# Four transposed chunks per PSUM bank in the first projection of a DiT block: earlier transposes, a reused bank, and one more split

## The chip, the cores, the metric

The kernel is one block of a diffusion transformer, written by hand for one core of one Trainium2 chip. The metric is the device time of one launch, in microseconds, lower is better. Every kernel here was correct against the reference. In all traces but one (x2_late, below) the granted clock, the share of full speed that the profile shows for the matrix engine, was 1.00 between 8.4 and 26 us, where the change lives.

Names: PE is the matrix engine (PEld its loading of weights), DVE the vector engine, ACT the scalar engine, POOL a further one; SP issues loads. PSUM is the memory into which the kernel's matmuls write, SBUF the one that holds their operands. A load "lands" when its last data have arrived.

## The reference, cut to what matters

```python
mod = (silu(c) @ w_mod).reshape(B, 6, 1, D)             # shift_a, scale_a, gate_a, ...
h   = layernorm(x) * (1 + scale_a) + shift_a            # B=2, N=256, D=1152
qkv = h @ wqkv                                          # k first in this kernel, then q, v
...                                                     # attention, wo, gate, second norm, MLP with F=4608
```

Only the first lines matter here. The kernel computes K from `layernorm(x) * (1 + scale_a)` while the weights are still arriving, and adds the shift later. D is nine chunks of 128, so the K projection is nine "K steps"; each needs one chunk of the normalized x, transposed, times its scale.

## The kernel before

The tokens are four tiles of 128: tiles 0 and 1 are batch 0, tiles 2 and 3 are batch 1. For each chunk the matrix engine transposes x into PSUM, DVE (batch 0) or ACT (chunk 1 and up, alternating) multiplies by the scale and writes `hT0` in SBUF, and the matrix engine multiplies `hT0` with six column blocks of `w_k`, accumulating in six PSUM banks. The two other banks are a rotating pair ("aux") for transposed chunks and for the scale matmuls (`scale_group`: nine matmuls of two columns per chunk).

```python
def scale_group(k0, k1, tile_of=aux_tile):              # pm = silu(c) @ w_scale for chunks k0..k1
    pm = tile_of([P, k1 - k0, B], "pm")
    ...                                                 # 9 matmuls of 2 columns per chunk
def modulate(pt, i, k, b, j0, eng):                     # hT0[chunk k, batch b] = pt * scale_a
    ...
# ---- the stage, in program order (cut) ----
pt_a = transpose_x([0, 1], BT[0])                       # chunks 0-1 of batch 0
act_mean_eps(2); act_root(2); root_exp(2, 3)            # statistics of token tile 2, on ACT
norm1(3, 0, CUT)
pm0, pm1 = [scale_group(k, k + 1, acc_tile) for k in range(2)]
...                                                     # hT0 chunks 0 and 1 of batch 0, on DVE
norm1(2, 0, CUT)                                        # DVE: x of tile 2, normalized, chunks 0-3
pt_c = aux_tile([P, 2, N], "pt", BF16)
transpose_x([0, 1], [3], pt_c, 1)                       # tile 3
fill(1)                                                 # one matmul on zeros, keeps the engine busy
k_step(0, 0, N)
k_step(1, 0, N, 0, 2)
transpose_x([0, 1], [2], pt_c, 0)                       # tile 2, the last to be normalized
k_step(1, 0, N, 2)
modulate(pt_c, 0, 0, 1, 0, "d"); modulate(pt_c, 1, 1, 1, 0, "a")
norm1(0, CUT, D); norm1(1, CUT, D)
k_step(0, N, T)
pm = scale_group(2, 4)
pt_b = transpose_x([2, 3], BT[0])
scale_add(pm, 2, 4)
modulate(pt_b, 0, 2, 0, 0, "d"); modulate(pt_b, 1, 3, 0, 0, "a")
norm1(2, CUT, D)
k_step(1, N, T)
pt_d = transpose_x([2, 3], BT[1])
...
k_step(2, 0, N); k_step(2, N, T)
for k in range(3, KD):
    split = 2 if k == 5 else 0
    k_step(k, 0, T, 0, split)                           # two of six column blocks first
    if k in (3, 5, 7):
        k1 = min(k + 3, KD)
        scale_add(scale_group(k + 1, k1), k + 1, k1)    # scales of the next two chunks
    if k < KD - 1:
        both(transpose_x([k + 1], range(NT)), k + 1)    # transposes, then DVE batch 0, ACT batch 1
    k_step(k, 0, T, split)
```

The loads of x (288 KB each) are the first on SP's queue, in the order tile 0, 1, 3, 2; the weights follow.

## Time and profile before

| | before |
|---|---|
| time, median of 6 runs | 243.49 us (243.23 to 243.89) |
| span of the profiled run | 241.4 us |
| matrix engine busy | 236.4 us, 98% |
| the stage of the change | 8.6 to 25.5 us |

From the page of the kernel before, the busy times and the chain that ended last:

```profile
PE 236.4 (98%) x1688; PEld 145.1 (60%) x1698; DVE 91.4 (38%) x193; ACT 59.9 (25%) x121; POOL 28.3 (12%) x47
...
PE 94%; issue 2%; ACT 2%; POOL 1%; DVE 0%; POOLq 0%; DVEq 0%; ACTq 0%
```

Busy time can't show whether the matrix engine waits, because matmuls overlap: each is listed for its whole passage. So I read start-to-start distances. Here is the timeline of PE of the kernel before, cut to the stretch that the change rewrites (columns: start in us, time until the end of the last of the group, engine, source line, operation, output<-inputs, shapes, count):

```profile
11.03 0.29 PE L264 MATMUL pt<-ident,xn 128*128 128x128 bf16 x2
11.15 1.42 PE L280 MATMUL pk<-big,w_k 128*128 128x256 bf16 x10
12.41 0.59 PE L247 MATMUL pm<-sT,w_scale_a 128*128 128x2 bf16 x18
12.86 0.38 PE L264 MATMUL pt<-ident,xn 128*128 128x128 bf16 x4
13.08 0.82 PE L280 MATMUL pk<-big,w_k 128*128 128x256 bf16 x6
13.74 0.39 PE L264 MATMUL pt<-ident,xn 128*128 128x128 bf16 x4
13.96 1.47 PE L280 MATMUL pk<-big,w_k 128*128 128x256 bf16 x12
15.27 0.59 PE L247 MATMUL pm<-sT,w_scale_a 128*128 128x2 bf16 x18
15.73 0.38 PE L264 MATMUL pt<-ident,xn 128*128 128x128 bf16 x4
...
17.24 0.39 PE L264 MATMUL pt<-ident,xn 128*128 128x128 bf16 x4
17.46 1.89 PE L280 MATMUL pk<-big,w_k 128*128 128x512 bf16 x8
```

One 256-column matmul of L280 is listed with 0.27 us, so twelve of them in 1.47 us start every (1.47 - 0.27) / 11 = 0.109 us. In the same way a transpose takes its turn of 0.055 us, a two-column matmul 0.025, a 512-column one 0.216. The Trainium skill, "TensorE: Matmul & The Clock Gate", section "Wait — 56ns, not 53.3ns?", gives N / 2.4 GHz + 2.5 ns and a floor of 25 ns; the trace agrees at all four sizes. Wherever the distance is longer, the engine waited. (In some groups a record is missing, and the distance doubles for that reason alone; those I leave out.) Read like this, the matrix engine of the kernel before waits 0.29 us ahead of the tile 2 transposes at 11.03, 0.17 us within the ten matmuls from 11.15.

Two landmarks will serve as a ruler: **the start of the tile 2 transposes** (11.03) and **the start of K step 4** (17.46), 6.43 us apart.

### The profile page before, as it was taken

How to read it: one execution, taken by the hardware profiler on the slowest of the kernel's cores; microseconds unless marked ns; L12 is line 12 of the kernel's file. 1: busy time of each engine (PE TensorE's matmuls, PEld its weight loads, DVE VectorE, ACT ScalarE, POOL GpSimd, SP SyncE). 2: the span in 40 equal slices, each digit the busy share in tenths (PEclk: the TensorE clock that was granted, in tenths of full speed). 3: DMA queues.
4: the chain of work that ended last, by engine and by line, in shares of the span. 5: the costliest groups of instructions: out<-in, count | busy, mean ns of one | idle time of the engine just before them, and what ended most of it. 6: DMA issues, size and time to landing. Idle time of an engine off the chain costs nothing.

```text
span 241.4 us, 3978 instructions
## 1 busy us (share of the span) xinstructions
PE 236.4 (98%) x1688; PEld 145.1 (60%) x1698; DVE 91.4 (38%) x193; ACT 59.9 (25%) x121; POOL 28.3 (12%) x47
## 2 busy tenths in 40 slices
PE   8999999999999999999999999999999999999994
PEld 5775444466667665888844444444665566666574
DVE  4842442319325678930003999950010000000001
ACT  6723322307215032770423333222000000000000
POOL 2300000001300324100000000001121111111111
PEclk9999999999999999999999999999999999999999
DMA  6999999997499993739999999999300000000000
GB/s 196 325 317 311 377 366 391 391 391 244 122 331 394 389 274 76 195 65 378 391 391 391 337 326 270 287 327 270 98 16 16 20 16 16 19 18 20 26 21 16
DMA packets 48781, 53.29 MB, mean 221 GB/s; under 512 B 9587, under 2 KB 36475, under 8 KB 48763
## 3 DMA queue, kind: packets, MB, share of 16 engines
q1 hardware_dynamic: 41312, 50.14, 62.5%
q10 hardware_dynamic: 6939, 1.71, 4.6%
q0 software_dynamic: 512, 1.19, 1.8%
q8 instruction: 13, 0.21, 0.4%
q14 instruction: 5, 0.04, 0.1%
HBM read 50.14 MB, written 1.19 MB: 213 GB/s over the span
## 4 chain that ended last, share of the span: by engine, by line
PE 94%; issue 2%; ACT 2%; POOL 1%; DVE 0%; POOLq 0%; DVEq 0%; ACTq 0%
PE pacc L802 29%; PE pacc L746 29%; PE pacc L693 7%; PE pacc L599 7%; PE pq L521 7%; PE pk L280 5%; PE pk L309 2%; PE pa L640 2%; PE ps_s L556 2%; PE pn L416 2%; ACT sink L206 1%; PE pt L264 1%; PE pm L247 1%; PE pg L498 0%; ACT rstd L335 0%
## 5 line engine op out<-in xcount | busy, mean ns | idle before, releaser
L746 PE MATMUL pacc<-hT,w_f 128*128 128x256 bf16 (+1 forms) x427 | 70.3, 325 | 0.3
L802 PE MATMUL pacc<-w_f,gT 128*128 128x384 bf16 (+2 forms) x468 | 70.5, 314 | 0.0
L802 PEld LDWEIGHTS <-gT 128*128 128x128 bf16 x468 | 44.4, 98 | 26.3
L746 PEld LDWEIGHTS <-w_f 128*128 128x128 bf16 x432 | 42.2, 98 | 27.6
L808 DVE TENSOR_TENSOR tmp<-pacc,gate 128x384 f32<-128x384 f32 (+2 forms) x13 | 6.8, 526 | 65.6 <-PE pacc L802 57.0
L778 ACT ACTIVATE gT<-pacc 128x512 bf16<-128x512 f32 x24 | 14.3, 597 | 32.7 <-PE pacc L746 32.7
L469 DVE SCALAR_TENSOR_TENSOR part<-w_gate_m,s,part 128x1152 f32<-128x1152 bf16 x16 | 21.4, 1412 | 0.0
L810 POOL TENSOR_TENSOR o_sb<-tmp,x 128x384 bf16<-128x384 f32 (+1 forms) x12 | 11.7, 972 | 53.9 <-DVE tmp L808 53.9
L693 PE MATMUL pacc<-w_o,big 128*128 128x384 bf16 x108 | 17.9, 326 | 0.0
L521 PE MATMUL pq<-hT,w_q 128*128 128x512 bf16 x79 | 17.7, 379 | 0.1
L599 PE MATMUL pacc<-w_v,hT 128*128 128x384 bf16 x108 | 17.7, 326 | 0.0
L599 PEld LDWEIGHTS <-hT 128*128 128x128 bf16 x108 | 10.5, 98 | 7.1 <-issue 0.2
L693 PEld LDWEIGHTS <-big 128*128 128x128 bf16 x108 | 10.4, 98 | 7.2 <-issue 0.4
L521 PEld LDWEIGHTS <-w_q 128*128 128x128 bf16 x81 | 7.8, 98 | 9.4
L280 PE MATMUL pk<-big,w_k 128*128 128x256 bf16 (+1 forms) x70 | 13.1, 324 | 0.1
L699 POOL TENSOR_TENSOR x<-tmp,x_sb 128x384 f32<-128x384 f32 x8 | 7.3, 912 | 27.0 <-DMA w_scale_m<-in_w_mod_dram 15.0
L467 DVE TENSOR_SCALAR part<-w_gate_m,s 128x1152 f32<-128x1152 bf16 x2 | 1.6, 818 | 21.9 <-DMA w_gate_m<-in_w_mod_dram 21.9
L491 POOL DMA_DIRECT2D gates_dram<-nat_v x2 | 1.1, 534 | 67.7 <-DVE nat_v L489 67.7
L280 PEld LDWEIGHTS <-w_k 128*128 128x128 bf16 x72 | 6.7, 97 | 3.7 <-issue 0.3
L767 ACT ACTIVATE gT<-pacc 128x512 bf16<-128x512 f32 x12 | 6.5, 598 | 9.1 <-PE pacc L746 9.1
L173 PE MATMUL pwarm<-zeros 128*128 128x256 f32 x18 | 7.4, 587 | 1.2 <-DVE eps_t L93 1.2
L512 POOL DMA_DIRECT2D gates_dram<-nat x4 | 2.4, 604 | 49.6 <-DVE nat L509 48.5
(102 smaller groups left out, 165.0 us busy)
## 6 DMA issues: line engine op xcount, KB each, us to landing
w_f<-in_w_fc_dram SPq DMA_DIRECT2D x12, 864.0 KB, 14.1
w_f<-in_w_fc_dram SPq DMA_DIRECT2D x3, 1728.0 KB, 7.9
w_f<-in_w_fc_dram SPq DMA_DIRECT2D x2, 2592.0 KB, 17.4
w_gate_a<-in_w_mod_dram SPq DMA_DIRECT2D x3, 864.0 KB, 12.1
w_v<-in_wqkv_dram SPq DMA_DIRECT2D x3, 864.0 KB, 13.8
w_o<-in_wo_dram SPq DMA_DIRECT2D x3, 864.0 KB, 14.0
w_shift_m<-in_w_mod_dram SPq DMA_DIRECT2D x3, 864.0 KB, 8.6
w_scale_m<-in_w_mod_dram SPq DMA_DIRECT2D x3, 864.0 KB, 13.3
```

The source lines that it names most:

```text
L173: nc.tensor.matmul(dst[:, 0:T // 2], zeros32[:, 0:P], zeros32, start=True, stop=True)
L280: nc.tensor.matmul(pk[m][:, c0:c1], w_k[:, k, m * P:(m + 1) * P], hT0[:, k, c0:c1], start=(k == 0 and c0 == 0), stop=(k == KD - 1), skip_g ...
L469: nc.vector.scalar_tensor_tensor(part[:, b, :], wg[:, k, :], s32[:, k, b:b + 1], part[:, b, :], op0=ALU.mult, op1=ALU.add,)
L521: nc.tensor.matmul(pq[m][:], w_q[:, k, m * P:(m + 1) * P], hT[:, k, :], start=(k == 0), stop=(k == KD - 1), skip_group_check=True,)
L599: nc.tensor.matmul(pacc[:], hT[:, k, t * P:(t + 1) * P], w_v[:, k, pnl * PW:(pnl + 1) * PW], start=(k == 0), stop=(k == KD - 1),)
L693: nc.tensor.matmul(pacc[:], aT[:, k, t * P:(t + 1) * P], w_o[:, k, c0:c1], start=(k == 0), stop=(k == KD - 1),)
L699: (nc.gpsimd if pool_add else nc.vector).tensor_tensor(x1[:, t, c0:c1], tmp[:], x_sb[:, t, c0:c1], op=ALU.add)
L746: nc.tensor.matmul(dst, w_f1[m // KD][:, k, ml * P:(ml + 1) * P], hT[:, k, c0:c1], start=start, stop=(k == KD - 1), **kw,)
L778: nc.scalar.activation(gT[:, m, :], pacc[:], ACT.Gelu_apprx_tanh)
L802: nc.tensor.matmul(pacc[:], gT[:, kk, t * P:(t + 1) * P], w_f2[j][:, r, c0 - n * PW:c0 - n * PW + cw], start=(kk == 0), stop=(kk == KF - 1),)
L808: nc.vector.tensor_tensor(tmp[:], pacc[:], gate_m[:, b, c0:c0 + cw], op=ALU.mult)
L810: (nc.vector if last else nc.gpsimd).tensor_tensor(o_sb[:], tmp[:], x1[:, t, c0:c0 + cw], op=ALU.add)
```

## The change

The intent: transpose chunks 2-3 together with chunks 0-1 while the matrix engine has to wait for tile 2 anyway, so that the work between tile 2 and K step 3 gets shorter. With four chunks of two tiles (4 x 256 bf16) the transposes fill a whole bank. There is then no bank left for the scales of chunks 2-3, so they go to a part of batch 0's bank that has been read already. The fill is halved, and K step 3 is split as K step 5 was.

```diff
@@ scale_group may be given its place; modulate returns its instruction; fill takes 256 columns, not 512 @@
-    pt_a = transpose_x([0, 1], BT[0])
+    pt_a = transpose_x([0, 1, 2, 3], BT[0])
...
-    pt_c = aux_tile([P, 2, N], "pt", BF16)
-    transpose_x([0, 1], [3], pt_c, 1)
+    pt_c = aux_tile([P, 4, N], "pt", BF16)
+    transpose_x([0, 1, 2, 3], [3], pt_c, 1)
...
-    modulate(pt_c, 1, 1, 1, 0, "a")
+    last_read = modulate(pt_c, 1, 1, 1, 0, "a")
...
     k_step(0, N, T)
-    pm = scale_group(2, 4)
-    pt_b = transpose_x([2, 3], BT[0])
-    scale_add(pm, 2, 4)
-    modulate(pt_b, 0, 2, 0, 0, "d")
-    modulate(pt_b, 1, 3, 0, 0, "a")
+    for i in (2, 3):
+        turn = nc.tensor.transpose(pt_c[:, i, 0:P], xns[2][:, i * P:(i + 1) * P], ident[:])
+        tc.add_manual_dep(turn.ins, last_read.ins.name, WAIT_FOR, reason="one engine per bank")
+    pm = pt_a[:, 0, 0:4 * B].bitcast(FP32).rearrange("p (j b) -> p j b", b=B)
+    scale_add(scale_group(2, 4, pm=pm), 2, 4)
+    modulate(pt_a, 2, 2, 0, 0, "d")
+    modulate(pt_a, 3, 3, 0, 0, "a")
+    modulate(pt_c, 2, 2, 1, 0, "d")
+    modulate(pt_c, 3, 3, 1, 0, "a")
     norm1(2, CUT, D)
+    norm1(3, CUT, D)
     k_step(1, N, T)
-    pt_d = transpose_x([2, 3], BT[1])
-    modulate(pt_d, 0, 2, 1, 0, "d")
-    modulate(pt_d, 1, 3, 1, 0, "a")
-    norm1(3, CUT, D)
...
-        split = 2 if k == 5 else 0
+        split = 2 if k in (3, 5) else 0
```

More of the change, by code (lines that the diff above doesn't have):

```diff
@@ L239, with scale_group @@
     scale_a = act.tile([P, KD, B], FP32, name="scale_a")
-    def scale_group(k0, k1, tile_of=aux_tile):
-        pm = tile_of([P, k1 - k0, B], "pm")
+    def scale_group(k0, k1, tile_of=aux_tile, pm=None):
+        if pm is None:
+            pm = tile_of([P, k1 - k0, B], "pm")
         for j in range(k0, k1):
@@ L269, in modulate @@
         if eng == "d":
-            nc.vector.tensor_scalar_mul(dst, src, sc)
-        else:
-            nc.scalar.mul(dst, src, sc)
+            return nc.vector.tensor_scalar_mul(dst, src, sc)
+        return nc.scalar.mul(dst, src, sc)
     pk = [None] * KD
@@ L322, in fill @@
         for _ in range(n):
-            nc.tensor.matmul(pwarm[:], zeros[:, 0:P], zeros[:], start=True, stop=True)
+            nc.tensor.matmul(pwarm[:, 0:N], zeros[:, 0:P], zeros[:, 0:N], start=True, stop=True)
     def pool_eps(t):
```

## The prediction

> **What bounds the kernel.** The matrix engine: the page has PE busy 236.4 of 241.4 us at granted clock 1.000, and the chain that ended last is 94% PE, two thirds of it the MLP, which the change doesn't touch. The change lives in the first projection stage, 8.6 to 25.5 us of the timeline. Matmuls overlap there, so I read start-to-start distances: 0.109 us for 256 columns, 0.216 for 512, 0.055 for a transpose, 0.025 for two columns (the Trainium skill, "TensorE: Matmul & The Clock Gate", gives N/2.4 GHz + 2.5 ns and a floor of 25 ns; the trace agrees). Against these PE really waits in four places: 0.29 us before the transposes of token tile 2 at 11.03 (for xn, behind ACT's root), 0.17 at 11.76 (DVE's chunk 0 of batch 1), 0.03 at 9.87, 0.05 at 21.00 (ACT's chunk 6).
>
> **What the change does.** No matmul disappears except half of the fill (0.11 us). Six transposes (0.33 us) move from behind 12.4 us to before 11.0 us: four of batch 0, two of tile 3.
>
> **Costs.**
> 1. Four more transposes at 8.61: the scale matmuls start at 9.27 instead of 9.05, chunk 0 of batch 0 is written 0.22 us later, K step 0 starts at about 10.08 (9.87 before). The two extra transposes of tile 3 are paid by the shorter fill.
> 2. This ends at 11.03: tile 2 waits for xn either way, and the 0.29 us hole shrinks to under 0.1. So far zero.
> 3. From 11.76 to K step 2: six fewer transposes, -0.33 us. But K step 1 now ends at about 13.6, while chunk 2 needs: scale matmuls end 12.98, +0.17 to the add, +0.27 to the multiply, +0.35 its duration, +0.05: about 13.82. New stall of about 0.2 us; before, transposes covered that latency. K step 2 ends at about 15.13 (15.27 before).
> 4. K step 3: before, the scale matmuls 4-5 waited about 0.03 us for weights that landed at 15.14. Two of six matmuls now go first and cover that. But behind the scale group only 1.30 us of PE work is left to hide the chain add-multiply-ACT, which took 1.36 us at K step 5, where the split exists already. New stall of about 0.06 us. K step 4 at about 17.38 (17.46 before).
> 5. After that nothing differs. Weights land 0.4 us or more ahead of use (w_q 31.57, used 32.00), so the shift carries through.
>
> **Sum:** -0.33 + 0.19 + 0.06, about -0.08 us on the critical path, 0.03% of the time. The before runs spread over 0.5 us, so it will be invisible in them.
>
> **Prediction:** 243.6 us, 243.1 to 244.1. Faster by over 2%: 0.5%; within 2%: 99%; slower by over 2%: 0.5%.
>
> **What would show it.** Tile 2 transposes still at about 11.03; K step 0 about 0.2 us later; a wait of about 0.2 us before K step 2, released by DVE's multiply; no wait for weights in K step 3; K step 4 0.05 to 0.15 us earlier; the Q projection at 31.9 instead of 32.0.
>
> **What would make it wrong.** The shared bank serialises more than I count: DVE and ACT take turns on a bank (ACT's idle time here ends with DVE's reads; the Trainium skill, "PSUM — Partial Sum Buffer", bank collisions, says that two engines on one bank collide), which could delay chunk 3. Or the stall at K step 2 is smaller: then the gain is up to 0.3 us. Or weights land later in some runs.

## The result, and the profile after

| | before | after |
|---|---|---|
| time, median of 6 runs | 243.49 us (243.23 to 243.89) | 243.43 us (243.15 to 244.05) |
| span of the profiled run | 241.42 us | 241.42 us |
| tile 2 transposes start | 11.03 | 11.20 |
| K step 4 starts | 17.46 | 17.48 |
| distance between the two | 6.43 | 6.28 |
| K step 4 to the end of the span | 223.96 | 223.94 |

The ratio after to before is 1.000, 95% interval 0.9983 to 1.0016. A ratio here is the mean time of one kernel's fast runs over that of the other's of the same rounds, so not quite the ratio of the medians. Executions over 1.5% slower than the fastest of the same kernel are left out of the means. No change of the time was measured: the interval is about 0.4 us wide to either side, so that the medians differ by 0.06 us says nothing.

The timeline of PE after, same stretch (asked for in windows, so the row at 13.15 ends with the matmuls that start by 15.14; the source lines moved down by one; L384 are the two late transposes of tile 2, and the scale matmuls L248 now write `pt`):

```profile
11.20 0.29 PE L265 MATMUL pt<-ident,xn 128*128 128x128 bf16 x2
11.33 1.42 PE L280 MATMUL pk<-big,w_k 128*128 128x256 bf16 x10
12.59 0.28 PE L384 MATMUL pt<-ident,xn 128*128 128x128 bf16 x2
12.70 0.59 PE L248 MATMUL pt<-sT,w_scale_a 128*128 128x2 bf16 x18
13.15 2.25 PE L280 MATMUL pk<-big,w_k 128*128 128x256 bf16 x18
...
15.67 0.59 PE L248 MATMUL pm<-sT,w_scale_a 128*128 128x2 bf16 x18
...
17.20 0.39 PE L265 MATMUL pt<-ident,xn 128*128 128x128 bf16 x4
17.48 1.89 PE L280 MATMUL pk<-big,w_k 128*128 128x512 bf16 x8
```

The two rows of four transposes at 12.86 and 13.74 have become one row of two: six fewer, 6 x 0.055 = 0.33 us. But the eighteen matmuls from 13.15 take 2.25 us; without a gap they would take 17 x 0.109 + 0.27 = 2.12. There is the new wait, 0.13 us, ahead of K step 2 (at 13.93). And K step 4 starts 0.28 us after the four transposes at 17.20, where 0.22 was enough before (17.24 to 17.46): another 0.05 us, before rounding. The sum is -0.33 + 0.13 + 0.05 = -0.15, just what the distance 6.43 to 6.28 shows.

So the stage did get shorter by 0.15 us. It also started 0.17 us later. The chain of waits says why. Before, in order of time (start, us, what):

```profile
7.02 0.20 ACT rstd L338
7.23 1.25 ACT sink L206 x2
8.50 1.36 ACT sink L206 x2
```

ACT came to the statistics of tile 2 (`sink`) from its own work. After:

```profile
2.09 5.17 DMA x_sb<-in_x_dram
...
7.29 1.36 ACT sink L206 x2
8.67 1.36 ACT sink L206 x2
```

In this execution the last load of x, tile 2, landed at 7.27 us (2.09 + 5.17) instead of 6.99, and ACT had to wait for it. The load is issued before anything that the change touches. It looked like the luck of one execution; the experiments had to show that.

### The profile page after: what moved, and what is told of

The parts are those of the page before. It is cut to its first block, busy times and chain, and to the rows that moved or that the text cites. A ratio compares the mean times of both kernels' runs of the same rounds, so it can differ in the third digit from the quotient of the medians.

```text
span 241.4 us, 3988 instructions
## 1 busy us (share of the span) xinstructions
PE 235.7 (98%) x1698; PEld 144.3 (60%) x1698; DVE 91.3 (38%) x193; ACT 59.9 (25%) x121; POOL 28.3 (12%) x47
## 4 chain that ended last, share of the span: by engine, by line
PE 94%; DMA 2%; ACT 1%; SPq 1%; DVE 0%; issue 0%; DVEq 0%; ACTq 0%
PE pacc L747 29%; PE pacc L803 29%; PE pacc L694 7%; PE pacc L600 7%; PE pq L522 7%; PE pk L280 5%; PE pk L309 2%; DMA x_sb<-in_x_dram 2%; PE pa L641 2%; PE ps_s L557 2%; PE pn L417 2%; ACT sink L206 1%; PE pt L265 1%; SPq L86 1%; PE pg L499 0%; PE pm L248 0%
## 5 line engine op out<-in xcount | busy, mean ns | idle before, releaser
L699 DVE TENSOR_TENSOR tmp<-pacc,gate 128x384 f32<-128x384 f32 x12 | 6.6, 549 | 3.1 <-PE pacc L694 3.1
```

What stands on the lines that cost most here:

```text
L699: nc.vector.tensor_tensor(tmp[:], pacc[:], gate_a[:, b, c0:c1], op=ALU.mult)
```

## The experiments

**The theories.** Theory A: the end of this kernel is the start of ACT's statistics of tile 2, plus a fixed chain to the tile 2 transposes, plus the distance from there to K step 4, plus a constant. The change shortens only the distance; the start jitters from run to run by more than that. Rival W: the arrival of the weights paces the stage, so that work removed from the matrix engine is given back at the next landing. (After 17.48 against before 17.46 fits W just as well.) A smaller rival, S, was that the split in K step 3 does all, or nothing, of the good. The halved fill was not tested alone; it lies ahead of the tile 2 transposes, so it is no part of the distance.

The table has the landmarks of all traces. "ACT" is the start of ACT's statistics of tile 2.

| run | ACT | tile 2 transposes | K step 4 | distance | K step 4 to end |
|---|---|---|---|---|---|
| before | 7.13 | 11.03 | 17.46 | 6.43 | 223.96 |
| before_again | 7.21 | 11.12 | 17.59 | 6.47 | 223.94 |
| split_only | 7.67 | 11.57 | 18.05 | 6.48 | 223.95 |
| after | 7.29 | 11.20 | 17.48 | 6.28 | 223.94 |
| after_again | 7.31 | 11.29 | 17.54 | 6.25 | 223.95 |
| turn_first | 7.40 | 11.31 | 17.58 | 6.27 | 223.99 |
| late4 | 7.35 | 11.26 | 17.75 | 6.49 | 223.94 |
| no_split3 | 7.20 | 11.10 | 17.72 | 6.62 | 224.12 |
| scale_first | 7.13 | 11.02 | 17.19 | 6.17 | 224.13 |
| x2_late | 9.53 | 13.59 | 20.44 | 6.85 | 223.94 |
| x2_late_fill | 9.07 | 12.99 | 19.26 | 6.27 | 223.94 |
| x2_act | 7.37 | 12.34 | 18.60 | 6.26 | 223.94 |
| half | 8.02 | 12.03 | 17.97 | 5.94 | 223.94 |
| half_again | 7.19 | 11.18 | 17.08 | 5.90 | 224.24 |

### 1. The two kernels once more

No edit.

> A null control: the kernel before, unchanged, a second trace. Theory A (the stage ends a fixed distance after token tile 2, whose start is set by when its x lands): transposes of tile 2 to K step 4 is 6.43 us again, K step 4 to the end of the span 223.9 us again; only the start of the tile 2 transposes moves, by the landing of x's tile 2 where that is later than ACT's free moment at about 7.2 us. Rival W (the landing of the weights paces the stage): K step 4 stays near 17.46 us whatever tile 2 does, so the distance 6.43 changes by as much as tile 2 moves. Time ratio 1.000 within 0.002.

> The changed kernel, unchanged, a second trace. Theory A: tile 2 transposes to K step 4 is 6.28 us again (0.15 less than before), with waits of 0.13 before K step 2 and 0.05 before K step 4; K step 4 itself is earlier than in the kernel before if x's tile 2 lands as early as there. Rival W: K step 4 at about 17.47 us again, whenever tile 2 starts. Time: ratio 0.998 to 1.001 under both, so the times alone decide nothing.

Measured: before_again has the distance 6.47 (6.43 expected; this time the scale matmuls of chunks 4-5 did wait 0.03 us for their weights, as the prediction had it), after_again 6.25. The medians were 243.54 and 243.31 us beside 243.53 of before; the ratios 0.9998 (0.9982 to 1.0013) and 0.9995 (0.9979 to 1.0011). Even an unchanged kernel can't be told from itself more finely than that, and 0.15 us is 0.06%.

In all eleven traces with unchanged loads (all but the two x2_late and x2_act) the tile 2 transposes start 3.89 to 4.01 us after ACT starts its statistics, and the end follows K step 4 by 223.94 to 224.24 us. That is theory A's sum. What delays ACT isn't always tile 2's own load: in split_only that landed at 7.10 us, but ACT came to it only at 7.67, after DVE had waited 0.5 us for tile 1's load (4.89 us, 4.34 in after). There was one thing I hadn't foreseen: in after_again the load of tile 3 landed late, at 6.52 us, DVE's queue was held up, and the first transposes started at 8.93 instead of 8.43. There the matrix engine came to tile 2 without a wait, 3.98 us after ACT instead of 3.91: the hole was gone altogether, and about 0.07 us of the extra early work was on the path. The hole that pays for the change isn't there in every execution.

### 2. The load of tile 2, later

```diff
-    for t in (0, 1, 3, 2):
+    for t in (0, 1, 3):
         nc.sync.dma_start(x_sb[:, t, :], ...)
...
     for k0, k1 in SGROUPS:
         nc.sync.dma_start(w_scale_a[...], ...)
+        if k0 == 0:
+            nc.sync.dma_start(x_sb[:, 2, :], x_v[:, 1, 0, :])
```

> The changed kernel with the load of x's tile 2 queued behind the first scale weights instead of ahead of them. It lands later by the time of that load, about 1.2 to 2 us. Theory A: the tile 2 transposes, K step 4 and the end of the kernel all move by as much as the landing moves (less up to 0.1 us), distance to K step 4 6.28 us again or slightly less, time +1 to +2 us (ratio 1.004 to 1.008). Rival W: the weights behind it land at the same time as ever, so K step 4 moves by much less than the landing, and the time by under 0.3 us.

Measured: the load landed at 9.51 us, 2.24 later than in after, and the time rose to 246.17 us, ratio 1.0109 (1.0095 to 1.0123), above the 1.004 to 1.008 expected. The start of tile 2 does set the end: W is refuted as the general rule, since the weights landed as ever (those for chunks 4-5 at 15.67 us, 15.37 after) while K step 4 moved by 2.96 us. But 2.96 is more than 2.24, and more than any theory had. The windows of this trace show the reason (columns: stretch, its length, then busy time and count for PE, PEld, DVE, ACT and POOL, granted clock, DMA share, GB/s):

```profile
9.86:11.46 1.60, 0.00 (x0) 0.00 (x0) 0.55 (x3) 1.57 (x3) 0.30 (x1) 1.00 1.19 306
11.46:15.20 3.74, 3.73 (x22) 2.77 (x23) 2.17 (x8) 1.77 (x5) 0.27 (x2) 0.54 1.14 322
```

For 1.60 us the matrix engine had nothing to do, because DVE waited 2.38 us, until 10.91, for ACT's first statistic of tile 2, and the normalization of tile 3 stands behind that in its program. After that hole the mean granted clock was 0.54 for 3.7 us (narrower windows give 1.00 up to 11.71, 0.50 from 11.72 to 15.12, then 1.00 again): 256-column matmuls started every 0.213 us instead of 0.109. All five runs of x2_late have a mean clock of 0.992 or 0.993, so it wasn't the luck of the traced one.

```diff
+    fill(14)                                            # in x2_late, ahead of tile 3's transposes
     transpose_x([0, 1, 2, 3], [3], pt_c, 1)
```

> The earlier variant with x's tile 2 loaded late (244.4 us span, matmuls at half speed from 11.9 to 15.2 us, granted clock 0.54 there), with 14 more fill matmuls of 256 columns in the hole before the transposes of tile 3. Theory C (the hole, by leaving the matrix engine idle, cost it its clock, and that cost about 0.7 us on top of the later landing): clock 1.00 all through, tile 2 transposes to K step 4 back at about 6.2 to 6.3 us (6.85 without the fill), time about 245.5 us instead of 246.2. Rival: the lower clock has another cause and stays; time 246.2 us or more.

Measured: distance 6.27, time 245.17 us (median of 4; before 243.61; ratio 1.007, 1.0021 to 1.0119). The window that had 0.54:

```profile
11.50:15.20 3.70, 3.29 (x46) 2.63 (x44) 1.80 (x6) 1.27 (x5) 0.00 (x0) 1.00 1.14 321
```

With work on zeros in the hole the clock stayed, and K step 4 came where theory A puts it, with this trace's start of ACT and the two distances of after: 9.07 + 3.91 + 6.28 = 19.26. In x2_late that sum was about 9.53 + 3.9 + 6.28 = 19.71, and it came at 20.44; the clock had cost 0.73 us. One of the four runs of x2_late_fill took 247.62 us, with a mean clock of 0.993, and one run of the kernel before 245.88, with 0.992, the figure of x2_late. They have no trace; it looks as if an unlucky landing can open such a hole in any of these kernels, but that was not shown.

### 3. The early transposes alone, undone

```diff
-    pt_a = transpose_x([0, 1, 2, 3], BT[0])
+    pt_a = aux_tile([P, 4, N], "pt", BF16)
+    transpose_x([0, 1], BT[0], pt_a)
...
         tc.add_manual_dep(turn.ins, last_read.ins.name, WAIT_FOR, reason="one engine per bank")
+    for j, t in enumerate(BT[0]):
+        for i in (2, 3):
+            nc.tensor.transpose(pt_a[:, i, j * P:(j + 1) * P], xns[t][:, i * P:(i + 1) * P], ident[:])
```

> The changed kernel with the four early transposes of batch 0 put back behind 12.4 us (right after the two late ones of tile 2), same bank, everything else as changed. Theory A: tile 2 transposes start no earlier than with the change (their start is set by x's tile 2), the hole before them grows by up to 0.2 us, and the distance to K step 4 grows by the four transposes, 6.28 + 0.22 = 6.50 us. Rival W (weights pace it): distance unchanged. Time: not visible.

Measured: 6.49. The timeline of PE shows the four transposes back on the path as a row of their own, with the work behind them moved by 0.22 us:

```profile
12.64 0.27 PE L385 MATMUL pt<-ident,xn 128*128 128x128 bf16 x2
12.75 0.39 PE L389 MATMUL pt<-ident,xn 128*128 128x128 bf16 x4
12.97 0.59 PE L248 MATMUL pt<-sT,w_scale_a 128*128 128x2 bf16 x18
13.43 2.03 PE L280 MATMUL pk<-big,w_k 128*128 128x256 bf16 x16
```

The tile 2 transposes started 3.91 us after ACT, as in after: the four transposes cost nothing early and their full 0.22 us late. So the removal is real, W fails here again, and without these four the rest of the change is worth nothing (6.49 against 6.43 to 6.47).

### 4. The split in K step 3

```diff
# no_split3: the change without its split
-        split = 2 if k in (3, 5) else 0
+        split = 2 if k == 5 else 0
# split_only: the kernel before with nothing but the split
-        split = 2 if k == 5 else 0
+        split = 2 if k in (3, 5) else 0
```

> The changed kernel with its second half undone: no split in K step 3, so the scale matmuls of chunks 4-5 come before all of K step 3, as in the kernel before. Theory A: the wait of 0.05 us before K step 4 goes away, but the scale matmuls now wait for their weights, which landed at 15.1 to 15.4 us in the traces so far, by 0.1 to 0.2 us; K step 4 comes 0.05 to 0.15 us later than with the split, counted from the tile 2 transposes (6.33 to 6.43 instead of 6.28). Rival S (the split is the useless half): distance 6.23 or less. Time: not visible.

> The kernel before with only the split in K step 3. Theory A: it removes a wait for weights of 0.03 us and makes one of 0.05 us before K step 4, so the distance from the tile 2 transposes to K step 4 stays at 6.43 to 6.48 us: alone it is worth nothing. Rival: the split carries the gain, distance about 6.28. Time: not visible.

Measured: split_only 6.48, as expected: alone it is worth nothing. no_split3 6.62, well above the 6.33 to 6.43 expected: I had the mechanism but not its size. The timeline of PE names the wait:

```profile
15.52 0.60 PE L248 MATMUL pm<-sT,w_scale_a 128*128 128x2 bf16 x18 [0.23 <-DMA w_scale_a<-in_w_mod_dram]
```

The bracket counts idle time after the modelled end of the last matmul; by start-to-start distance the wait is 0.40 us. The weights landed at 15.47 us, and tile 2 happened to be early in this execution (11.10), so the matrix engine stood at them sooner than in the traces from which I had estimated. Sum: 6.28 - 0.05 + 0.40 = 6.63. Here W is right: once the matrix engine is 0.15 us faster, it would run into this landing, and the split covers it with two matmuls of 0.216 us each, for a price of 0.05. But 0.40 is the size in this one trace, which was not repeated: the weights landed 4.37 us after the start of the tile 2 transposes, the latest of the eleven (3.98 to 4.31 in the others, 4.17 in after). With 4.17 the wait would be about 0.20 us and the distance about 6.43, an estimate from these numbers and again no better than before. So neither half of the change is good without the other, by a margin that one landing decides.

K step 4 to the end is 224.12 us here, 0.18 more than usual. The first weights of the Q projection landed at 32.36 us (30.43 to 31.91 in all other traces), and the projection started at 32.41, 14.69 us after K step 4 instead of 14.54.

### 5. Why the new wait was 0.13 and not 0.19 us

The prediction had put 0.27 us between DVE's add (scales of chunks 2-3) and the first multiply that uses them. DVE's timeline before, and then after:

```profile
13.04 0.16 DVE L257 TENSOR_SCALAR scale_a<-pm 128x4 f32<-128x4 f32 x1 [0.62 <-PE pm L247]
13.31 0.35 DVE L270 TENSOR_SCALAR big<-pt,scale_a 128x256 bf16<-128x256 bf16 x1
```

```profile
13.33 0.16 DVE L258 TENSOR_SCALAR scale_a<-pt 128x4 f32<-128x4 f32 x1 [0.73 <-PE pt L248]
13.53 0.35 DVE L271 TENSOR_SCALAR big<-pt,scale_a 128x256 bf16<-128x256 bf16 x1
```

0.20 us instead of 0.27. In the trace before, a separate wait instruction (at 13.24 us) stands ahead of this multiply, since it must wait for two semaphores, its own add's and the transposes'. After the change the transposes are long known to be done, and it waits for one. The Trainium skill, "Perfetto Trace Analysis", section "Identifying Dependency Chains", says that such extra instructions may be inserted; what one costs it doesn't say. The rival was that reading the bank just read makes the difference. The test puts the transposes of chunk 8 ahead of the scale matmuls of chunk 8, in two banks:

```diff
         k_step(k, 0, T, 0, split)
+        early_pt = transpose_x([k + 1], range(NT)) if k == 7 else None
         if k in (3, 5, 7):
             ...                                         # scale matmuls
         if k < KD - 1:
-            both(transpose_x([k + 1], range(NT)), k + 1)
+            both(early_pt or transpose_x([k + 1], range(NT)), k + 1)
```

> The changed kernel with the transposes of chunk 8 ahead of the scale matmuls of chunk 8 instead of behind them. This tests why the multiply followed the add by 0.20 us at K step 2 in the changed kernel and by 0.27 us elsewhere. Theory A (one semaphore wait less: the transposes are already known to be done, so the multiply waits for the add alone): 0.20 us here too, and no separate wait instruction ahead of it. Rival B (it comes from reading the bank just read by the add): here scale and transposes are in two banks, so 0.27 us as before. K step 8 without a wait under A, with one of about 0.07 us under B.

Measured, first the kernel after and then turn_first, DVE's and ACT's timeline at chunk 8:

```profile
22.71 0.16 DVE L258 TENSOR_SCALAR scale_a<-pm 128x2 f32<-128x2 f32 x1 [1.20 <-PE pm L248]
22.98 0.35 DVE L271 TENSOR_SCALAR big<-pt,scale_a 128x256 bf16<-128x256 bf16 x1
23.36 0.47 ACT L272 ACTIVATE big<-pt,scale_a 128x256 bf16<-128x256 bf16 x1 [1.34 <-DVE big L271]
```

```profile
23.04 0.16 DVE L258 TENSOR_SCALAR scale_a<-pm 128x2 f32<-128x2 f32 x1 [1.42 <-PE pm L248]
23.23 0.35 DVE L271 TENSOR_SCALAR big<-pt,scale_a 128x256 bf16<-128x256 bf16 x1
23.68 0.47 ACT L272 ACTIVATE big<-pt,scale_a 128x256 bf16<-128x256 bf16 x1 [1.55 <-DVE big L271]
```

Add to multiply is 0.27 us in after and 0.19 in turn_first, without a wait instruction and with two banks: the number of semaphores decides, not the bank. The second half of the expectation missed. K step 8 waited 0.05 us, not zero, because the 0.07 us came back one engine on: multiply to ACT's start is 0.38 us in after and 0.45 in turn_first, and the trace has the extra wait instruction in front of ACT now (at 23.61 us).

### 6. The scales before the late transposes

```diff
+    pm = scale_group(2, 4, pm=pm)                       # ahead of the two late transposes of tile 2
     for i in (2, 3):
         turn = nc.tensor.transpose(pt_c[:, i, 0:P], ...)
-    scale_add(scale_group(2, 4, pm=pm), 2, 4)
+    scale_add(pm, 2, 4)
```

> The changed kernel with the scale matmuls of chunks 2-3 ahead of the two late transposes of tile 2 instead of behind them. Theory A: the chain add, multiply, K step 2 starts 0.11 us earlier, the wait before K step 2 falls from 0.13 to about 0.02, tile 2 transposes to K step 4 falls from 6.28 to 6.17 us. Rival W: the distance doesn't fall, because K step 2 or 3 then waits for its weights. Time: no visible difference.

Measured: 6.17, and the wait ahead of K step 2 is gone (eighteen matmuls in 2.14 us, 2.25 after):

```profile
12.41 0.59 PE L248 MATMUL pt<-sT,w_scale_a 128*128 128x2 bf16 x18
12.86 0.27 PE L386 MATMUL pt<-ident,xn 128*128 128x128 bf16 x2
12.97 2.14 PE L280 MATMUL pk<-big,w_k 128*128 128x256 bf16 x18
...
17.19 1.89 PE L280 MATMUL pk<-big,w_k 128*128 128x512 bf16 x8
19.10 0.60 PE L248 MATMUL pm<-sT,w_scale_a 128*128 128x2 bf16 x18
```

But K step 4 to the end is 224.13 us, 0.19 more than usual. The scale weights of chunks 6-7 landed at 19.05 us in this execution (18.17 to 18.82 in the traces of the two kernels and of experiments 3 to 5), and the matmuls that need them stood at 19.10. All of the extra gain was given back one landing later. One look, no timing; it shows how near the weights are behind.

### 7. Two attempts at more

```diff
# x2_act: x's tile 2 on ACT's queue, where it was issued at 1.38 instead of 2.09 us
-        nc.sync.dma_start(x_sb[:, t, :], ...)
+        (nc.scalar if t == 2 else nc.sync).dma_start(x_sb[:, t, :], ...)
```

> The changed kernel with the load of x's tile 2 issued from ACT's queue at the start instead of fourth from SP. Theory A: it lands earlier than the 6.5 to 7.4 us of the traces so far, ACT's statistics of tile 2 then start when ACT is free, at about 7.15 instead of 7.3 us, and the tile 2 transposes and K step 4 come 0.1 to 0.2 us earlier, the distance between them unchanged at 6.28 us; time -0.1 to -0.2 us, hardly visible. Rival: the four tiles share one bandwidth, so all land at about 7 us and tile 1's or 3's normalization is late instead: no gain or a loss.

Measured: the rival was right in the traced execution. Tile 2 landed at 7.35 us, no earlier than usual, and tile 3, the third on SP's queue, only at 7.57 (5.75 in after); the chain of waits runs through tile 3 and DVE's statistics to the first transposes, 1.5 us later than in after:

```profile
1.63 5.93 DMA x_sb<-in_x_dram
7.59 1.49 DVE stats L193 x3
...
9.98 0.62 PE pt L265 x8
```

That execution took 244.32 us; the three others 243.13 to 243.44. The ratio is 0.998 (0.994 to 1.002): nothing to be told from noise.

```diff
# half: on top of scale_first; tile 3's half of K steps 0-1 is done while tile 2 is still normalized
+    modulate_tile(3, 0, "d"); read3 = modulate_tile(3, 1, "a")     # 128 columns each
     norm1(2, 0, CUT)
     ...
+    k_step(0, 3 * P, T)                                 # tile 3 alone, ahead of tile 2's transposes
     ...                                                 # tile 2's transposes, now behind read3
     k_step(1, 0, N, 2)
+    k_step(1, 3 * P, T)
-    modulate(pt_c, 0, 0, 1, 0, "d"); last_read = modulate(pt_c, 1, 1, 1, 0, "a")
+    modulate_tile(2, 0, "d"); last_read = modulate_tile(2, 1, "a")
...
-    k_step(0, N, T)
     pm = scale_group(2, 4, pm=pm)
+    k_step(0, N, 3 * P)
...
-    k_step(1, N, T)
+    k_step(1, N, 3 * P)
```

> An attempt at more: the variant with the scale matmuls first, and with the two K steps of batch 1's token tile 3 done alone (128 columns) while tile 2 is still being normalized. Theory A alone would give: the holes before the tile 2 transposes (0.27 us) and before K step 0 of batch 1 (0.17 us) are filled, and K step 4 comes up to 0.5 us earlier than in the changed kernel. Theory A with the weights behind it: weights for K steps 2-3 land at 13.0 to 13.5 us and for scale chunks 4-5 at 15.0 to 15.6 us in the traces, and from those the chain to K step 4 takes about 1.8 us, so K step 4 comes no earlier than about 17.2 us: at most 0.3 us earlier than in the changed kernel, with new waits for weights of 0.1 to 0.5 us in K steps 2 or 3. Time: -0.1 to -0.3 us, ratio 0.9985 to 1.000.

> The same kernel as half, unchanged: its first trace fell on an execution whose x tile 2 landed at 8.00 us, the latest of all the ordinary traces, and the call's runs of before had one at 245.88 us, so neither trace nor ratio was typical. With tile 2 landing at 6.9 to 7.4 us: the tile 2 transposes at 11.0 to 11.3 us; Theory A with the weights behind it: new waits for weights before the scale matmuls of chunks 4-5 of 0.2 to 0.5 us, so K step 4 starts at about 1.8 us after those weights land (17.0 to 17.3 us), instead of the 5.7 us after tile 2 that the filled holes alone would give. Time: ratio 0.9985 to 0.9995, within the noise.

Measured: distance 5.94 and 5.90 us, 0.34 to 0.38 us less than in after. The hole ahead of tile 2 is filled. But in half_again the matrix engine now stands before the weights of chunks 2-3 (0.10 us by start-to-start distance, at 12.16), 4-5 (0.11 us) and 6-7 (0.26 us). The 0.11 is less than the 0.2 to 0.5 expected; the bracket below shows 0.17 because one of the two split matmuls ahead of it, which start at 14.71, is missing from the trace (15.26 - 14.71 - 2 x 0.216 = 0.11). From the timeline of PE and the list of waits, which counts the idle time of the weight loads, also longer than the wait itself (columns there: who waited for whom, us in total, times, longest):

```profile
15.26 0.60 PE L248 MATMUL pm<-sT,w_scale_a 128*128 128x2 bf16 x18 [0.17 <-DMA w_scale_a<-in_w_mod_dram]
```

```profile
PEld L248 <- DMA w_scale_a<-in_w_mod_dram: 1.0, 2, 0.6
```

K step 4 came at 17.08 us, 1.87 after those weights landed (15.21), within the 17.0 to 17.3 expected; and of this lead 0.3 us went at the next landing (K step 4 to end 224.24). Times: half 243.44 us beside 243.61, ratio 0.997 (0.994 to 1.000); half_again 243.25 beside 243.49, ratio 0.9991 (0.9979 to 1.0003). It has the lower median both times, and its interval holds 1 both times. I don't call it faster.

## Why the prediction was right, point by point

- **The time: 243.6 us predicted, 243.43 measured, no change beyond noise.** Right, and for the reason given: a gain of the order of 0.1 us on the critical path against a spread of more than half a microsecond. The time alone could not have told this reason from another; the distances do.
- **Six transposes off the path, -0.33 us.** Right; late4 puts four of them back and pays 0.22 us.
- **The extra early transposes are paid by the hole ahead of tile 2.** Right in after: the tile 2 transposes start 3.91 us after ACT, as in before_again. But that K step 0 came at 10.07 us, with 10.08 predicted, was luck. The first transposes started at 8.43 instead of 8.61, and the scale matmuls then waited about 0.15 us for their weights, which landed at 9.20; the prediction has no such wait. The timeline of PEld in after shows it:

```profile
9.24 0.52 PEld L248 LDWEIGHTS <-w_scale_a 128*128 128x128 bf16 x18 [0.17 <-DMA w_scale_a<-in_w_mod_dram]
```

  The hole isn't left over in every execution: in after_again the hole was used up and 0.07 us showed.
- **A new wait of 0.19 us ahead of K step 2.** Right in place and cause, too large: 0.13. The term that was mis-sized is "+0.27 to the multiply", which measured 0.20, because that multiply needs one semaphore wait less.
- **A new wait of 0.06 us ahead of K step 4.** Right: 0.05.
- **The weights wait in K step 3.** The split does cover it, but the wait was put at 0.03 us, which only before_again shows (in the trace of before the matmuls from 13.96 fill the time to 15.27); in the faster kernel without the split it was 0.40 (no_split3), about 0.20 with a usual landing. It isn't in the sum, so the sum didn't suffer.
- **Sum -0.08 us.** Measured -0.15, by the distance from tile 2 to K step 4.
- **"Tile 2 transposes still at about 11.03, Q projection at 31.9."** Wrong in the trace: 11.20 and 32.01. I took one trace's landing of x for a fixed time. Over the ordinary traces with the loads as they are, ACT started tile 2 between 7.13 and 8.02 us, and everything behind moves with it.
- **"After that nothing differs; weights land 0.4 us or more ahead of use."** The first half held for the change itself (K step 4 to end within 0.02 us). The margin didn't: in after_again the first weights of the Q projection landed at 31.91 us and were used at 32.08, in no_split3 the projection waited for them, and scale_first and half_again gave 0.2 to 0.3 us back to the weights of chunks 6-7.
- **"The shared bank serialises more than I count", with chunk 3 late.** Not seen: in after K step 3 started at 15.24 us, straight behind K step 2.

What stays open: why the loads of x land up to a microsecond apart from execution to execution, and what the runs of 245.88 and 247.62 us, which have no trace, went through.

## What to carry to other kernels

Where the path is a race of several arrivals, measure a change by the distance between two landmarks in the trace, not by the clock time at which something happens: the start of the stretch may jitter by more than the gain. Work moved off the path into an idle hole is gained only until the next thing that used to be hidden shows up, so list the latencies that the removed work had been covering, and the landings behind them, before summing. And do count semaphore waits: moving a producer earlier can take a wait instruction off the chain, or merely hand it to the next engine.

## What the Trainium skill lacked or had wrong

- "TensorE: Matmul & The Clock Gate", sections "What's actually happening" and "HAM oscillation": they tie the loss of the full clock to an idle window of about 3.4 us. In x2_late the longest stretch without any matmul was 1.62 us (another of 1.23 ended at 8.58 us), and yet the clock was at half speed from 11.72 to 15.12 us, which cost 0.73 us. This doesn't show the page wrong: from 7.35 to 11.46 us the engine ran only eight transposes and nineteen matmuls of two columns, and whether such work counts against idleness was not tested. What these two sections lack is how much work keeps the clock; fourteen 256-column matmuls in the hole were enough (1.00 in x2_late_fill). The rates themselves agree with the page: 0.213 us for 256 columns at half speed, 0.109 at full.
- "Perfetto Trace Analysis", section "Identifying Dependency Chains", mentions the extra wait instructions but no cost; they took 0.07 us each here, on DVE (0.27 against 0.20 us from add to multiply) and on ACT (0.45 against 0.38 from multiply to ACT's start).
- None of the pages that I read says how far apart the same load can land in executions of one program: x's tile 2, issued fourth at the start, landed between 6.49 and 8.00 us in the eleven traces with unchanged load order.
